# mLSTM and two-level expert layer on one core: first scores moved ahead of the end of the gate sums, gate tanh in 24 pieces, carried states in four tiles

## The chip, the cores and the metric

One NeuronCore of a Trainium2 chip runs the whole program. The metric is the device time of one execution in microseconds; a kernel's time is the median over several executions.

## What is computed

Two stages follow each other. An mLSTM (4 batches, 8 heads, 768 tokens, head size 40) makes one row of 320 numbers per token; 3072 such rows then go through a mixture of 16 experts, of which each token uses one.

```python
for t in range(S):                       # mLSTM, per batch and head
    m_new = max(f_gate[t] + m, i_gate[t])
    f_stab = exp(f_gate[t] + m - m_new); i_stab = exp(i_gate[t] - m_new)
    C = f_stab * C + i_stab * outer(v[t], k[t])
    n = f_stab * n + i_stab * k[t]
    y[t] = sigmoid(o_gate[t]) * (C @ q[t]) / max(abs(n @ q[t]), 1)
x = y as (3072, 320)
g = argmax(x @ w_group); e = argmax(x @ w_expert[g])
out = softmax_g * softmax_e * (relu(x @ w1[g, e]) @ w2[g, e])
```

## The kernel before

**Units.** The first stage does the recurrence in chunks of 128 tokens. One unit u is chunk c = u // 4 of batch b = u % 4, with all 8 heads, so there are 24 units, done in order. Inside a chunk the recurrence is a masked product, as in attention; across chunks each batch and head carries a state of 40 by 41 numbers (the extra column is n).

**What a unit does**, with the names that the profile shows:

- `scores(u)` (L218): TensorE makes keys times queries into the two PSUM tiles `sp`. Needs the transfer of `qk`.
- `decay(u, r)` for r = 0 and 1: `aprod` (L188, L191) makes four 128x128 decay exponents with TensorE into a PSUM bank `aw`, and `exps` (L201) turns them on ScalarE into half r of `ab` with four exponentials. In chunk 0 a matmul of `neg_b` (L188) comes first and masks. The pool `ps_a` has one buffer: a second `aw` can only be written when the four exponentials of the one before have read it. Three calls early in the program take the bank tagged `lg` instead.
- `masked(u, r)` (L223): VectorE multiplies `sp` by `ab` into `pt`.
- `carried(u)` (L243), from chunk 1 on: TensorE multiplies the queries by the carried state, read from `Cflat`, into the tile `it`. `carried2` (L250, VectorE) scales it by `eacol`. `it` also has one buffer; `state(u)` (L262) writes the chunk's contribution into its second half, and `state2(u)` (L277, L279; VectorE, one unit later) adds that to the state. `decayed(u)` (L269, GpSimd) scales the state.
- `values(u)` (L290): TensorE makes `av` from `pt` and the values `nt`.
- `norm1`, `rows`, `rows2` (L296 to L319), for unit u - 1: VectorE and GpSimd normalise and multiply by the output gate `sig`, giving `x`. `store` (L333, L334) copies a strip on ScalarE and writes the rows to DRAM. `turn` (L327, L350) transposes `x` on TensorE into the bank `tp` and copies it to `xT` on ScalarE. The bank `tp` too is single, and the gate sums use it as well.
- `gate_o(c)` (L169): tanh of the output gates of a chunk's four units in one ScalarE instruction of 128x1280, in place.

**Order.** Units 0 to 21 stand in an order written out by hand (`unit`), and each engine runs its own instructions in that order; a scheduler places only what comes after. In unit u stand, in this order: loads for u + 3, scores(u), the last part of unit u - 1, masked(u), carried(u), keyw(u + 1) (L230, GpSimd), decay(u + 2, 0), turn(u - 1), values(u), state(u), decay(u + 2, 1). After decay(u + 2, 1) of units 2, 6, 10, 14 and 18 comes `gate_o` of the next chunk.

**The start.** `gate_sums(0)` (L964 on) makes the cumulative gates of chunk 0 in five steps on VectorE and GpSimd, and last a transpose on TensorE into `tp` (L988) that gives `bcol`, the exponentials' bias. Before it TensorE runs 11 matmuls on ones (`busy`, L133). After it come decay(0, 0), decay(0, 1), scores(0), the rest of unit 0, then `unit(1, first=True)`, which also does both halves of decay(2). `gate_sums(1)` and `later_sums` do the later chunks' gates in between; after unit 2, and again after unit 6, `ends` (L1005) makes a matmul into `tp`, from which ScalarE makes `decs` with two copies (L1008).

After unit 23 the experts run, from L764 to L871 mostly; weights arrive in halves, are split into a rounded part and a rest, and three products are summed.

Of the kernel before, what the change touches and what calls it, by code (L numbers as in the profile page):

```python
# [7 lines left out]
F32 = mybir.dt.float32  # L8
# [3 lines left out]
AF = mybir.ActivationFunctionType  # L12
# [6 lines left out]
P = 128  # L19
B, H, S, D = 4, 8, 768, 40  # L20
NCH = S // P
NU = NCH * B
# [12 lines left out]
D1 = D + 1  # L35
Z = 64 - D
KS = 64 + D
HC = 4 * D1
# [26 lines left out]
def lstm_moe(ctx: ExitStack, tc: tile.TileContext, gates, qkT, nat, og, wcat, w1, w2, cst, out):  # L65
    nc = tc.nc
    enter = ctx.enter_context
    mm = nc.tensor.matmul
# [39 lines left out]
    ap_ = att_pool("att", 1)  # L108
# [2 lines left out]
    Apc = ap_.tile([P, S], BF16, name="Apc")  # L111
    sel_b = ap_.tile([P, B * H], BF16, name="sel_b")
    decs = ap_.tile([P, NCH, B * 4], F32, name="decs")
    Cflat = ap_.tile([P, B * HC + P - D1], F32, name="Cflat")
    Cst = Cflat[:, 0:B * HC].rearrange("p (a e) -> p a e", e=D1)
    kws = [ap_.tile([P, 4 * KS + Z], F32, name=f"kw{i}") for i in range(2)]
    rows_of = slice(0, 64), slice(64, 64 + D)
    bcol = ap_.tile([P, NCH, B * H], F32, name="bcol")
# [1 line left out]
    wk = att_pool("wk", 2)  # L120
# [40 lines left out]
    sigs = {}  # L161
# [3 lines left out]
        nc.sync.dma_start(t, og[:, c * B:(c + 1) * B, :])  # L165
        sigs[c] = t

    def gate_o(c):
        nc.scalar.activation(sigs[c], sigs[c], AF.Tanh, scale=0.5)  # L169

    def upper(a, fill):
        rt["mask"] = nc.gpsimd.affine_select(out=a, in_=a, pattern=[[0, a.shape[1]], [1, P]], compare_op=ALU.is_ge, fill=fill,
# [30 lines left out]
    def decay(u, r, **kw):  # L203
        aprod(u, r, **kw)
        exps(u, r)
# [5 lines left out]
    def scores(u):  # L211
        t = st_[u]
        qk = t["qk"]
        t["pm"] = [ps_s.tile([P, 4, P], F32, name="sp") for _ in range(2)]
        for pr in range(4):
            for r in range(2):
                rs = rows_of[r]
                mm(t["pm"][r][:, pr, :], qk[rs, 0, pr, :], qk[rs, 1, pr, :], start=True, stop=True)  # L218
# [15 lines left out]
    def carried(u):  # L234
        c, b = divmod(u, B)
        t = st_[u]
        it = t["it"] = ps_a.tile([P, 2, 512], F32, name="it")
        if c > 0:
            for pr in range(4):
                for r in range(2):  # L240
                    rs = rows_of[r]
                    o = (b * 4 + pr) * D1
                    mm(it[:, r, pr * D1:pr * D1 + P], t["qk"][rs, 1, pr, :], Cflat[rs, o:o + P], start=True, stop=True)  # L243

    def carried2(u):
        c, b = divmod(u, B)
# [18 lines left out]
    def decayed(u):  # L265
        c, b = divmod(u, B)
        if 0 < c < NCH - 1:
            cb = Cst[:, b * 4:b * 4 + 4, :]
            nc.gpsimd.tensor_tensor(cb, cb, bc(decs[:, c, b * 4:b * 4 + 4].unsqueeze(2), (P, 4, D1)), op=ALU.mult)  # L269

    def state2(u):
        c, b = divmod(u, B)
        if c < NCH - 1:
            st = st_[u]["it"][:, 1, HC:2 * HC].rearrange("p (a e) -> p a e", e=D1)
            cb = Cst[:, b * 4:b * 4 + 4, :]
            if c > 0:
                nc.vector.tensor_tensor(cb, cb, st, op=ALU.add)  # L277
            else:
                nc.vector.tensor_copy(cb, st)  # L279
# [58 lines left out]
    def turn(u):  # L338
        x = st_[u]["x"]
        tp = ps_1.tile([P, 3, P], F32, name="tp", tag="tp")  # L340
        ins = turned(tp, x, (0, P, DM - P))
        rt["tp", u] = ins
        if NU - 4 < u < NU - 1:
            with tc.issue_after(ins.ins):
                busy(2 if u == NU - 3 else 1)
        if u == NU - 1:
            xT = lasting().rearrange("p (k c) -> p k c", k=3)
        else:
            xT = wk.tile([P, 3, P], F32, name="xT", bufs=5)
        nc.scalar.copy(xT, tp)  # L350
        st_[u]["xT"] = xT
        if NU - 4 < u < NU - 1:
            with tc.issue_after(ins.ins):
                do(early_turns, 1)
# [526 lines left out]
    def run(stage, u):  # L881
        if 0 <= u < NU:
            stage(u)
# [12 lines left out]
    def unit(u, more=0, first=False):  # L896
        run(loads, u + 3)
        if u == 6:
            first_tokens()
        if u == 9:  # L900
            last_rows()
        if u % B == 1 and u // B + 1 < NCH:
            load_o(u // B + 1)
        with ExitStack() as st:
            if u == MANUAL:
                st.enter_context(tc.issue_after(rt["av", u - 1].ins))
            run(scores, u)
        if first:
            decay(2, 0)
            decay(2, 1, pool=ps_1, tag="lg")  # L910
        with ExitStack() as st:
            if u == NU:
                st.enter_context(tc.high_priority())
            run(norm1, u - 1)
            run(rows, u - 1)
            run(state2, u - 1)
            run(rows2, u - 1)
        if u in (17, 19, 20, 21):
            put_id()
        run(store, u - 1)  # L920
        run(mask, u + 1)
        run(lambda v: masked(v, 0), u)
        run(lambda v: masked(v, 1), u)
        run(carried, u)
        run(decayed, u)
        run(carried2, u)
        if u == MANUAL:
            with tc.issue_after(rt["num"].ins):
                go_on(9, "B")
        run(keyw, u + 1)  # L930
        run(lambda v: decay(v, 0), u + 2)
        if u < NU:
            run(turn, u - 1)
        if u < NU - 1:
            go_on(9 if u < MANUAL else 0, "A")
        elif u == NU - 1:
            with tc.issue_after(rt["tp", u - 1].ins):
                go_on(1, "A")
            with tc.issue_after(rt["num"].ins):
                go_on(3, "B")  # L940
            with tc.issue_after(rt["mask"].ins):
                while ids:
                    put_id()
            logits(u - 2)
            logits(u - 1)
            go_on(4, "B")
        if u == 5:
            first_rows()
        run(values, u)
        run(state, u)  # L950
        if u in ROUTE:
            logits_of(ROUTE[u], 0, B)
        run(lambda v: decay(v, 1), u + 2)
        if u < MANUAL:
            go_on(4 + more, "B")
        if u in ROUTE:
            logits_back(ROUTE[u], 0, B)
        if u % B == 2 and u // B + 1 < NCH:
            gate_o(u // B + 1)
        if u < MANUAL:  # L960
            put_id()

# [80 lines left out]
    def sum_on(n=1):  # L1043
        for _ in range(n):
            if sums and next(sums[0], StopIteration) is StopIteration:
                sums.pop(0)

    with tc.manual_schedule():
        nc.sync.dma_start(G[:, 0], gates[0:BH])
        nc.scalar.dma_start(cs, cst)  # L1050
        nc.scalar.dma_start(G[:, 1], gates[BH:2 * BH])
        nc.scalar.dma_start(G4, gates[2 * BH:])
        nc.vector.memset(ones_b, 1.0)
        nc.vector.memset(sep, 0.0)
        nc.scalar.activation(sep, sep, AF.Exp)
        busy(11)
        nc.vector.memset(ones4, 1.0)
        nc.vector.memset(Dl[:, 0, 0:1], 0.0)
        nc.vector.memset(Apc[96:P], 0.0)
        for t in qkp[0:2]:  # L1060
            nc.gpsimd.memset(t[0:Z], 0.0)
        load_qk(0)
        loads(0)
        load_o(0)
        load_qk(1)
        loads(1)
        loads(2)
        nc.scalar.copy(sel_b, cs[:, C_SEL:C_SEL + B * H])
        nc.scalar.copy(lt_b, cs[:, C_LT:C_LT + P])
        nc.scalar.activation(neg_b, ident, AF.Copy, scale=NEG)  # L1070
        sums.append(gate_sums(0))
        sum_on(9)
        for t in kws:
            nc.gpsimd.memset(t, 0.0)
        nc.gpsimd.memset(zero_b, 0.0)
        for t in qkp[2:]:
            nc.gpsimd.memset(t[0:Z], 0.0)
        nc.gpsimd.memset(Cflat, 0.0)
        nc.gpsimd.tensor_copy(id_b, ident)
        decay(0, 0)  # L1080
        decay(0, 1, pool=ps_1, tag="lg")
        scores(0)
        keyw(0)
        masked(0, 0)
        masked(0, 1)
        carried(0)
        carried2(0)
        sums.append(gate_sums(1))
        decay(1, 0)
        values(0)  # L1090
        gate_o(0)
        decay(1, 1, pool=ps_1, tag="lg")
        state(0)
        sum_on(3)
        keyw(1)
        nc.gpsimd.iota(tokid, pattern=[[P, NBLK], [0, IW]], base=0, channel_multiplier=1)
        nc.gpsimd.tensor_copy(keyb, cs[:, C_15E:C_15E + NE])
        nc.gpsimd.tensor_copy(base_b, cs[:, C_BASE:C_BASE + NE])
        nc.gpsimd.memset(ohsum[0], 0.0)
        loads(3)  # L1100
        nc.sync.dma_start(wc, wcat)
        unit(1, first=True)
        sum_on(9)
        sums.append(later_sums())
        sum_on(1)
        for u in range(2, 10):
            unit(u)
            do(due if u in (2, 6) else [])
            sum_on({2: 2, 3: 3, 4: 2, 5: 9}.get(u, 0))
# [113 lines left out]
    with tc.For_i(0, nv, 1):  # L1223
# [6 lines left out]
        v = wk2.tile([P, 3], F32, name="v")  # L1230
# [30 lines left out]
        for f in range(NF):  # L1261
            ps = pools["ps_h"].tile([P, 512], F32, name="psh")
            for k in range(3):
                kk = min(P, DM - k * P)
                mm(ps[:, 0:P], w1s[0:kk, k * F + f * P:k * F + (f + 1) * P], xT[0:kk, k, :], start=(k == 0),
                   stop=(k == 2))
# [74 lines left out]
```

## Time and profile before

| what | value |
|---|---|
| median of 3 executions | 391.44 us (389.32 to 392.74) |
| the profiled execution's own time | 389.26 us |
| its span in the profile | 387.7 us |
| TensorE busy | 368.8 us (95%) |
| VectorE busy | 274.1 us (71%) |
| ScalarE busy | 212.1 us (55%) |
| GpSimd busy | 171.1 us (44%) |
| granted TensorE clock, mean | 0.994 |

The profile is of one execution, 1.56 us longer by its own time than its span. PE is TensorE's matmuls, PEld its weight loads, DVE VectorE, ACT ScalarE, POOL GpSimd, SPq the queue that issues most transfers. In a timeline row stand start, length, engine, line, output and inputs; "[idle before <-releaser]" is how long that engine had nothing to run and what ended last before it. An fp32 matmul shows as two records, so 8 of them read x16. The first stage ends around 150 us.

### The profile page before, as it was taken

How to read it: one execution, taken by the hardware profiler on the slowest of the kernel's cores; microseconds unless marked ns; L12 is line 12 of the kernel's file. 1: busy time of each engine (PE TensorE's matmuls, PEld its weight loads, DVE VectorE, ACT ScalarE, POOL GpSimd, SP SyncE). 2: the span in 40 equal slices, each digit the busy share in tenths (PEclk: the TensorE clock that was granted, in tenths of full speed). 3: DMA queues.
4: the chain of work that ended last, by engine and by line, in shares of the span. 5: the costliest groups of instructions: out<-in, count | busy, mean ns of one | idle time of the engine just before them, and what ended most of it. 6: DMA issues, size and time to landing. Idle time of an engine off the chain costs nothing.

```text
span 387.7 us, 9816 instructions
## 1 busy us (share of the span) xinstructions
PE 368.8 (95%) x3688; PEld 339.9 (88%) x3688; DVE 274.1 (71%) x702; ACT 212.1 (55%) x533; POOL 171.1 (44%) x222
## 2 busy tenths in 40 slices
PE   7989999999999999877999999999999999999994
PEld 4778988979978888877999898999999998888993
DVE  5867876898898976786697767865755666656620
ACT  5664574565746532435675556755746745455520
POOL 7545486566767434374433216352141243141310
PEclk9999999999999999998999999999999999999999
DMA  7976856899795731149952369995862718988700
GB/s 230 264 244 171 206 164 193 301 325 280 208 332 133 221 85 44 15 121 356 374 181 65 103 249 385 407 319 199 315 229 80 265 43 318 332 342 294 251 18 10
DMA packets 29553, 84.05 MB, mean 217 GB/s; under 512 B 12168, under 2 KB 16754, under 8 KB 25922
## 3 DMA queue, kind: packets, MB, share of 16 engines
q1 hardware_dynamic: 24258, 66.41, 52.1%
q0 software_dynamic: 4912, 16.66, 12.7%
q8 instruction: 29, 0.48, 0.5%
q10 hardware_dynamic: 336, 0.36, 0.3%
q14 instruction: 18, 0.15, 0.1%
HBM read 73.11 MB, written 10.54 MB: 216 GB/s over the span
## 4 chain that ended last, share of the span: by engine, by line
PE 63%; issue 13%; DVE 11%; DMA 7%; POOL 2%; ACT 2%; POOLq 1%; SPq 0%; DVEq 0%; ACTq 0%
PE psh L816 13%; PE av L290 8%; PE po L857 5%; PE po L855 5%; PE po L856 5%; PE sp L218 4%; PE it L243 4%; PE tpm L327 2%; PE aw L191 2%; PE it L262 2%; DVE w2l L682 2%; PE tp L327 2%; DMA w2s<-in_w_dram 2%; PE psh L764 1%; DMA ix<-itab 1%
## 5 line engine op out<-in xcount | busy, mean ns | idle before, releaser
L201 ACT ACTIVATE ab<-aw,bcol 128x128 f32<-128x128 f32 x192 | 54.5, 371 | 41.9 <-PE aw L191 38.9
L622 POOL DMA_INDIRECT out_dram<-y,ix x32 | 38.1, 1190 | 88.9 <-ACT y L867 72.7
L855 PE MATMUL po<-w2h,hh 128*128 128x320 f32 (+3 forms) x200 | 63.4, 317 | 0.0
L857 PE MATMUL po<-w2h,hh 128*128 128x320 f32 (+3 forms) x200 | 62.2, 311 | 1.1 <-DVE hh L753 1.1
L856 PE MATMUL po<-w2l,hh 128*128 128x320 f32 (+3 forms) x200 | 61.9, 309 | 0.0
L618 POOL DMA_INDIRECT xg<-x_d,ix x32 | 34.3, 1073 | 49.2 <-DMA ix<-itab 27.2
L816 PE MATMUL psh<-xhl,w1hl 128*128 128x240 f32 (+5 forms) x336 | 54.0, 287 | 0.4 <-DVE hf L748 0.4
L682 DVE TENSOR_TENSOR w2l<-w2s,w2h 128x640 fp32r<-128x640 f32 x52 | 41.3, 833 | 15.4 <-ACT w2h L680 13.3
L750 ACT ACTIVATE hh<-psh 128x256 fp32r<-128x256 f32 (+5 forms) x68 | 28.8, 429 | 40.5 <-DVE hf L748 20.0
L753 DVE SCALAR_TENSOR_TENSOR hh<-psh,hh 128x256 fp32r<-128x256 f32 (+4 forms) x76 | 31.9, 442 | 24.0 <-ACT hh L750 22.8
L290 PE MATMUL av<-nt,pt 128*128 128x128 f32 x384 | 47.7, 276 | 0.5 <-DVE pt L223 0.5
L816 PEld LDWEIGHTS psh<-xhl,w1hl 128*128 128x128 f32 x336 | 46.3, 189 | 1.5 <-PE psh L816 0.9
L290 PEld LDWEIGHTS av<-nt,pt 128*128 128x128 f32 x384 | 45.1, 192 | 1.1 <-DVE pt L223 0.9
L223 DVE TENSOR_TENSOR pt<-sp,ab 128x512 f32<-128x512 f32 x48 | 30.9, 684 | 11.7 <-PE sp L218 11.1
L857 PEld LDWEIGHTS po<-w2h,hh 128*128 128x128 f32 (+3 forms) x200 | 36.6, 183 | 1.4 <-DVE hh L753 1.4
L855 PEld LDWEIGHTS po<-w2h,hh 128*128 128x128 f32 (+3 forms) x200 | 36.8, 184 | 0.5 <-ACT y L867 0.5
L867 ACT ACTIVATE y<-po,xg 128x320 f32<-128x320 f32 (+3 forms) x25 | 13.2, 529 | 43.9 <-PE po L857 43.7
L856 PEld LDWEIGHTS po<-w2l,hh 128*128 128x128 f32 (+3 forms) x200 | 36.8, 184 | 0.0
L764 PE MATMUL psh<-xhl,w1s 128*128 128x144 f32 (+7 forms) x336 | 36.0, 284 | 0.0
L680 ACT CAST w2h<-w2s 128x640 fp32r<-128x640 f32 x52 | 35.0, 724 | 0.9 <-DMA w2s<-in_w_dram 0.9
L764 PEld LDWEIGHTS psh<-xhl,w1s 128*128 128x128 f32 (+1 forms) x336 | 34.4, 190 | 1.1 <-issue 0.2
L526 POOL DMA_INDIRECT itab<-tokid,slot x24 | 25.7, 1070 | 17.5 <-DVE slot L449 7.5
(229 smaller groups left out, 728.6 us busy)
## 6 DMA issues: line engine op xcount, KB each, us to landing
w1s<-in_w_dram SPq DMA_DIRECT2D x12, 1536.0 KB
w2s<-in_w_dram SPq DMA_DIRECT2D x9, 1280.0 KB
nt<-in_nat_dram SPq DMA_DIRECT2D x24, 324.0 KB
qk<-in_qkT_dram SPq DMA_DIRECT2D x24, 320.0 KB
x_d<-x SPq DMA_DIRECT2D x23, 192.0 KB
sig<-in_og_dram SPq DMA_DIRECT2D x6, 640.0 KB
w1hl<-in_w_dram SPq DMA_DIRECT2D x3, 1280.0 KB
w1s<-in_w_dram SPq DMA_DIRECT2D x4, 768.0 KB
```

The lines of the kernel that those rows point to most:

```text
L201: rt["exp"] = nc.scalar.activation(st_[u]["ab"][:, r, j, :], aw[:, j, :], AF.Exp, bias=bcol[:, c, i:i + 1])
L290: ins = mm(av[:, i:i + P], t["pm"][r][:, pr, :], nt[:, o:o + P], start=True, stop=True)
L618: return nc.gpsimd.indirect_dma_start(out=o, out_offset=None, in_=src, in_offset=bass.IndirectOffsetOnAxis(ap=idx, axis=0))
L622: return nc.gpsimd.indirect_dma_start(out=out, out_offset=bass.IndirectOffsetOnAxis(ap=idx, axis=0), in_=y, in_offset=None, bounds_check=N ...
L680: nc.scalar.copy(a, src[:, s])
L682: lows.append(lambda: nc.vector.tensor_tensor(o[rows], src[rows, s], a[rows].bitcast(F32), op=ALU.subtract))
L753: rt['low'] = nc.vector.scalar_tensor_tensor(hh[:, f:f + per, dst], src[:, :, t], 0.0, hr.bitcast(F32)[:, :, t], op0=ALU.max, op1=ALU.subt ...
L764: return mm(banks[i][:, g * W1:(g + 1) * W1], w1s[rs, s:s + P], xhl[rs, k, :], **kw)
L816: ins = mm(ps[:, g * W1:(g + 1) * W1], w[:, s], x, start=(n == 0), stop=(n == len(todo) - 1))
L855: mm(po[0:m], hh[:, f, t], w2h[:, s], start=st0, stop=False)
L856: mm(po[0:m], hh[:, f, t], w2l[:, s], start=False, stop=False)
L857: ins = mm(po[0:m], hh[:, f, tl], w2h[:, s], start=False, stop=sp0)
```

## The change

1. The gate sums of chunk 0 run their five steps, then `scores(0)` is emitted, then the last step, the transpose and `bcol`. Before, scores(0) came after the transpose and after both halves of decay(0).
2. `gate_o` takes a unit instead of a chunk: one tanh of 128x320 per unit, 24 in all instead of 6. Unit 0's and unit 1's stand where their unit is written; from unit 1 on each unit u also does unit u + 1's, between its state matmuls and decay(u + 2, 1).
3. In unit 1 alone, values(1) and state(1) come ahead of turn(0) and decay(3, 0).
4. The carried states lie in four tiles, one for each batch, of 251 columns each, instead of one of 743. Each is cleared by its own memset.
5. `xT` has 4 buffers instead of 5.

```diff
-    Cflat = ap_.tile([P, B * HC + P - D1], F32, name="Cflat")
-    Cst = Cflat[:, 0:B * HC].rearrange("p (a e) -> p a e", e=D1)
+    Cst = [ap_.tile([P, HC + P - D1], F32, name=f"Cst{i}") for i in range(B)]
...
-    def gate_o(c):
-        nc.scalar.activation(sigs[c], sigs[c], AF.Tanh, scale=0.5)
+    def gate_o(u):
+        c, b = divmod(u, B)
+        nc.scalar.activation(sigs[c][:, b], sigs[c][:, b], AF.Tanh, scale=0.5)
...
-                    o = (b * 4 + pr) * D1
-                    mm(it[:, r, pr * D1:pr * D1 + P], t["qk"][rs, 1, pr, :], Cflat[rs, o:o + P], start=True, stop=True)
+                    o = pr * D1
+                    mm(it[:, r, o:o + P], t["qk"][rs, 1, pr, :], Cst[b][rs, o:o + P], start=True, stop=True)
...
-            xT = wk.tile([P, 3, P], F32, name="xT", bufs=5)
+            xT = wk.tile([P, 3, P], F32, name="xT", bufs=4)
...
         run(keyw, u + 1)
-        run(lambda v: decay(v, 0), u + 2)
-        if u < NU:
-            run(turn, u - 1)
+        if not first:
+            run(lambda v: decay(v, 0), u + 2)
+            if u < NU:
+                run(turn, u - 1)
...
         run(values, u)
         run(state, u)
+        if first:
+            turn(u - 1)
+            decay(u + 2, 0)
+            gate_o(u)
+        run(gate_o, u + 1)
...
-        if u % B == 2 and u // B + 1 < NCH:
-            gate_o(u // B + 1)
...
         sums.append(gate_sums(0))
+        sum_on(5)
+        scores(0)
         sum_on(9)
...
-        nc.gpsimd.memset(Cflat, 0.0)
+        for t in Cst:
+            nc.gpsimd.memset(t, 0.0)
         nc.gpsimd.tensor_copy(id_b, ident)
         decay(0, 0)
         decay(0, 1, pool=ps_1, tag="lg")
-        scores(0)
```

**TensorE at the start**, after the 11 matmuls on ones; `sp` is scores(0), `tp` the transpose for `bcol`, `aw` the decays of unit 0 and, at the end, of unit 1.

```order
-L988 MATMUL tp<-cs,G 128x32
...
+L218 MATMUL sp<-qk_93 128x128 x8
+L992 MATMUL tp<-cs,G 128x32
 L188 LDWEIGHTS lt_b
 L188 MATMUL aw<-neg_b,lt_b 128x512
...
 L191 LDWEIGHTS sel_b
 L191 MATMUL aw<-Apc,sel_b 128x128
-L218 MATMUL sp<-qk_93 128x128 x8
 L188 LDWEIGHTS lt_b
```

The eight score matmuls stood behind both decays and now stand ahead of the transpose.

**TensorE in unit 1**, behind the decays of unit 2; `av` is values(1), `it` state(1), `tp` turn(0), and the two `aw` groups are decay(3, 0) and decay(3, 1).

```order
 L191 LDWEIGHTS sel_b
 L191 MATMUL aw<-Apc,sel_b 128x128
+L290 MATMUL av<-nt,pt 128x128 x8
+L262 MATMUL it<-nt,kw_105 64x41 x8
+L327 MATMUL tp<-cs,x 128x128 x3
 L188 LDWEIGHTS lt_b
...
-L327 MATMUL tp<-cs,x 128x128 x3
-L290 MATMUL av<-nt,pt 128x128 x8
-L262 MATMUL it<-nt,kw_102 64x41 x8
 L188 LDWEIGHTS lt_b
 L188 MATMUL aw<-neg_b,lt_b 128x512
```

turn(0), values(1) and state(1) stood between the two halves of decay(3); now all three stand ahead of both, and the halves follow each other directly.

**ScalarE from unit 1's copy of `xT` to the copies of `decs` after unit 2.** `ab` are groups of four exponentials. First as it was:

```order
L350 COPY xT<-tp 128x384
L201 ACTIVATE ab<-aw,bcol 128x128 x4
L998 ACTIVATE eacol<-tp 128x32
L999 COPY bcol<-tp 128x32
L333 COPY x<-x 128x64
L201 ACTIVATE ab<-aw,bcol 128x128 x4
L350 COPY xT<-tp 128x384
L201 ACTIVATE ab<-aw,bcol 128x128 x4
L169 ACTIVATE sig<-sig 128x1280
L1008 COPY decs<-tp 64x16 x2
```

Now the exponentials of decay(3, 0) come behind `xT`:

```order
L350 COPY xT<-tp 128x384
L201 ACTIVATE ab<-aw,bcol 128x128 x4
L169 ACTIVATE sig<-sig 128x320 x2
L201 ACTIVATE ab<-aw,bcol 128x128 x4
L1002 ACTIVATE eacol<-tp 128x32
L1003 COPY bcol<-tp 128x32
L333 COPY x<-x 128x64
L201 ACTIVATE ab<-aw,bcol 128x128 x4
L350 COPY xT<-tp 128x384
L169 ACTIVATE sig<-sig 128x320
L201 ACTIVATE ab<-aw,bcol 128x128 x4
L1012 COPY decs<-tp 64x16 x2
```

The tanh of a whole chunk no longer stands between the exponentials and the copies of `decs`; two small ones stand between the exponentials of decay(3, 0) and of decay(3, 1), and one ahead of those of decay(4, 1). The tanh of the last unit, 23, lies outside the hand-written order; the scheduler puts it on ScalarE in unit 17, right behind that of unit 18. On TensorE, VectorE, GpSimd and SP nothing else changes its place.

## Prediction before the result

> **What bounds the kernel now.** The page first: the engines' busy time and the chain of work that ended last.
>
> ```profile
> PE 368.8 (95%) x3688; PEld 339.9 (88%) x3688; DVE 274.1 (71%) x702; ACT 212.1 (55%) x533; POOL 171.1 (44%) x222
> PE 63%; issue 13%; DVE 11%; DMA 7%; POOL 2%; ACT 2%; POOLq 1%; SPq 0%; DVEq 0%; ACTq 0%
> ```
>
> TensorE is busy nearly throughout, and ScalarE, which most of the change touches, holds 2% of the chain. A reordering can win only what TensorE stands idle in the first stage. The busy time by stages tells how much that is; the start's row:
>
> ```profile
> 5.20:27.00 21.80, 19.04 (x227) 15.97 (x227) 15.76 (x45) 15.08 (x52) 12.29 (x23) 1.00 0.96 273
> ```
>
> The second column is the length of the stretch, the third TensorE's busy time in it: 2.76 us idle between 5.2 and 27 us, at the full granted clock (1.00). The waits of TensorE name the holes, first those of 13 to 28 us, then those of 27 to 130 us: a wait, its sum, its count, the longest.
>
> ```profile
> PE tp L327 <- POOL ab L172: 1.0, 1, 1.0
> PE aw L188 <- ACT ab L201: 0.8, 1, 0.8
> ```
>
> ```profile
> PE it L243 <- DVE Cflat L277: 1.5, 4, 0.6
> PE tp L327 <- POOL x L319: 0.2, 1, 0.2
> ```
>
> So there are two holes near the moved instructions, 0.8 and 1.0 us, and later a third kind, 1.5 us in four pieces, before the matmuls on the carried state. The change touches the surroundings of all three.
>
> **Part A, scores(0) ahead.** The start, from the timelines of TensorE, SP, ScalarE and VectorE, and what SP's queue waited for:
>
> ```profile
> 1.26 3.98 PE L133 MATMUL busy<-ones_b 128*128 128x512 bf16 x11 [1.26 <-DVE sep L1054]
> 5.41 0.24 PE L988 MATMUL tp<-cs,G 32*128 32x32 f32 x1 [0.16 <-POOL G L977]
> 5.58 0.39 PE L188 MATMUL aw<-neg_b,lt_b 128*128 128x512 bf16 x1
> 6.26 0.38 PE L191 MATMUL aw<-Apc,sel_b 128*128 128x128 bf16 x4 [0.29 <-POOL Apc L985]
> 7.02 1.16 PE L218 MATMUL sp<-qk 64*128 64x128 f32 x16
> 8.11 0.39 PE L188 MATMUL aw<-neg_b,lt_b 128*128 128x512 bf16 x1
> 8.34 0.39 PE L191 MATMUL aw<-Apc,sel_b 128*128 128x128 bf16 x4
> 9.03 2.05 PE L290 MATMUL av<-nt,pt 128*128 128x128 f32 x16 [0.31 <-DVE pt L223]
> 10.92 0.38 PE L188 MATMUL aw<-neg_b,lt_b 128*128 128x512 bf16 x1
> 5.05 0.33 SPq L181 DMA_DIRECT2D nt<-in_nat_dram  x1
> SPq L181 <- DMA qk<-in_qkT_dram: 0.3, 1, 0.3
> 6.68 3.22 ACT L201 ACTIVATE ab<-aw,bcol 128x128 f32<-128x128 f32 x12 [2.20 <-PE aw L191]
> 8.29 1.30 DVE L223 TENSOR_TENSOR pt<-sp,ab 128x512 f32<-128x512 f32 x2 [2.00 <-PE sp L218]
> ```
>
> The matmuls on ones end at 1.26 + 3.98 = 5.24. SP's issue at 5.05 had waited for the transfer of the first keys, so these lie ready at about 5.0, just in time. scores(0) then runs from 5.24 for 1.09 (7.02 to 8.11), to 6.33. The transpose, until now at 5.41, goes to 6.33. The masking matmul follows it 0.17 later (5.41 to 5.58), the decay that 0.23 later (8.11 to 8.34) where it need not wait for the gates, as it did at 6.26; by 6.7 these are long ready. So the first decay runs from 6.73 to 7.11, where it was done at 6.64, and the exponentials begin at 7.15 instead of 6.68. Four of them take 1.14, so the first product `pt` can begin at 8.33, against 8.29 when it waited for the scores. The second needs all eight (2.17, from the row of eight below) and begins at 9.36, where it began 0.65 after the first, at 8.94. From a product's start to the matmuls that await it pass 0.74 (8.29 to 9.03). values(0) starts at 9.07, is half through after 0.95 (half of 9.03 to 10.92), at 10.02, then waits for the second `pt` until 10.10, and ends at 11.04 instead of 10.92. **Part A: 0.1 us lost**, and VectorE 0.45 us behind. Bounds: 0.2 won if the second product is not awaited; 1.8 lost (7.02 - 5.24) if the keys are not there before 7.02, which is all that the old place proves by itself. I take the 0.1, since SP's wait dates the keys.
>
> **Part B, unit 1.**
>
> ```profile
> 9.50 0.51 DVE L969 TENSOR_TENSOR_SCAN M__126<-G,M__126 32x128 f32<-32x128 f32 x1
> 13.24 1.29 DVE L223 TENSOR_TENSOR pt<-sp,ab 128x512 f32<-128x512 f32 x2
> 13.79 2.17 ACT L201 ACTIVATE ab<-aw,bcol 128x128 f32<-128x128 f32 x8 [1.09 <-PE aw L191]
> 14.99 0.38 PE L188 MATMUL aw<-neg_b,lt_b 128*128 128x512 bf16 x1 [0.79 <-ACT ab L201]
> 15.76 1.95 PE L290 MATMUL av<-nt,pt 128*128 128x128 f32 x16
> 17.64 0.67 PE L262 MATMUL it<-nt,kw 128*64 128x41 f32 x16
> 18.24 0.39 PE L188 MATMUL aw<-neg_b,lt_b 128*128 128x512 bf16 x1
> 19.02 1.16 PE L218 MATMUL sp<-qk 64*128 64x128 f32 x16
> 16.95 0.56 ACT L350 COPY xT<-tp 128x384 f32<-128x384 f32 x1
> ```
>
> Until now decay(3, 0) waited 0.79 for the single bank `aw`, held until the first four exponentials of unit 2 were through (13.79 + 1.14). values(1), state(1) and turn(0) now go into that gap. But VectorE bounds values(1): from L969 to the product `pt` it worked 3.74 us without a pause (9.50 to 13.24), and it now begins 0.45 late, so `pt` starts at 13.70 and, with the 0.74, values(1) at 14.44. It takes 1.88 and state(1) 0.60 (from start to start above), turn(0) 0.36 (26.65 to 27.01 in part C): 17.28. decay(3, 0) is done 0.23 + 0.39 later, at 17.90. And now the same bank bites harder: decay(3, 1) comes next, with nothing between, and must wait for four exponentials, from 17.95 (after the copy of `xT`) to 19.09. It starts at 19.15, 0.06 behind them as at 14.99, and scores(2) 0.78 later as before, at 19.93 instead of 19.02. **Part B: with A 0.91 lost, so 0.81 by itself.** The work that used to hide this wait (turn, values and state, 2.8 us) stands before it now. Bounds: the wait cannot shrink below the 1.14 of the exponentials, so without any slip on VectorE 0.6 is lost; with the 0.56 of `xT` wholly in front of them, 1.3.
>
> The tanh of units 1 and 2 stands between those exponentials and the next four. From the slope between the 1286 ns of 1280 columns and the 371 of 128 (rows in part D), 320 columns take 0.52 us, and 0.41 from start to start. Two put the exponentials of decay(3, 1) at 19.8 to 20.9; decay(4, 0) wants their bank at 21.0, behind scores(2). That hides them, barely.
>
> The Trainium skill (ScalarE: Activation LUTs, Rules for kernel authors) budgets about 0.3 us per ACTIVATE plus 0.83 ns an element, which speaks against cutting one into four; an estimate from it is 0.57 for a piece. By that budget the two pieces would end 0.3 later and the sum would come out 0.2 to 0.3 us slower than by the rows. The trace agrees on the long form (1.29 against 1.36), but starts short ones every 0.26 us (twelve in 3.22), so the row's figure is the one I use.
>
> **Part C, no long tanh after unit 2.**
>
> ```profile
> 24.04 1.14 ACT L201 ACTIVATE ab<-aw,bcol 128x128 f32<-128x128 f32 x4 [1.94 <-PE aw L191]
> 25.05 1.29 ACT L169 ACTIVATE sig<-sig 128x1280 f32<-128x1280 f32 x1
> 26.21 0.34 ACT L1008 COPY decs<-tp 64x16 f32<-64x16 f32 x2
> 24.22 0.72 POOL L319 TENSOR_TENSOR x<-xn,den 128x320 f32<-128x320 f32 x1 [3.38 <-DVE xn L310]
> 25.23 0.39 PE L191 MATMUL aw<-Apc,sel_b 128*128 128x128 bf16 x4
> 25.39 1.29 DVE L223 TENSOR_TENSOR pt<-sp,ab 128x512 f32<-128x512 f32 x2 [1.01 <-PE sp L218]
> 26.65 0.52 PE L327 MATMUL tp<-cs,x 128*128 128x128 f32 x3 [1.03 <-POOL ab L172]
> 27.01 1.95 PE L290 MATMUL av<-nt,pt 128*128 128x128 f32 x16
> ```
>
> The profile names GpSimd's mask for the 1.03 us. It is another: turn(2) needs `x`, done at 24.94, and the bank `tp`, which the `decs` copies held to 26.55; they stood behind the tanh. That tanh goes. All this is 0.91 late from part B: turn(2) could start at 25.62 + 0.91 = 26.53 (the end of decay(5, 0)), and the copies end at 24.95 + 1.01 + 0.34 = 26.30, so it does not wait. values(3) now waits for its `pt` instead: 25.39 + 0.91 + 0.74 = 27.04. It used to start at 27.01. **Part C gives back 0.88 of 1.03**; more than that only if `pt` were earlier, and nothing if something else held turn(2) to its old delay.
>
> **Part D, what costs nothing.**
>
> ```profile
> L169 ACT ACTIVATE sig<-sig 128x1280 f32<-128x1280 f32 x6 | 7.7, 1286 | 0.0
> L201 ACT ACTIVATE ab<-aw,bcol 128x128 f32<-128x128 f32 x184 | 52.2, 371 | 40.1 <-PE aw L191 37.1 <-PE tp L327 2.5 <-ACT x L333 0.3
> L1078 POOL MEMSET Cflat<- x1: 707/707/707, 9.0 to 9.0; 128x743 f32 x1
> ```
>
> 24 pieces at 0.41 are 9.8 us of ScalarE against 7.0 for six at 1.16: 2.8 us more. Each stands just ahead of exponentials before which ScalarE idled, 40.1 us in 46 groups, so they are hidden; without that cover the 18 after unit 4 would cost up to 7. The other long ones win nothing by going: after 27 us TensorE waits for no ScalarE row. Four memsets clear 1004 columns for 743, some 0.3 us at the 707 ns, ahead of the weighted keys that state(0) awaits; those have as much slack, and if not, state(0) moves by 0.1. The fifth `xT` buffer was never needed: the logits of a chunk read its four ahead of the next turn.
>
> The state tiles free nothing either. carried(u) waits for L277 of the unit before, of another batch. But `it`, which it writes, has one buffer, and the same L277 reads it: the wait stays. Bounds: 0, and 1.5 won.
>
> **Sum.** +0.10 + 0.81 - 0.88 = +0.03 us, that is none, on the profiled execution's 389.26. That one lay 2.2 below the median of the runs shown; the difference carried to the median gives **391.4**. The terms' bounds give -0.4 to +1.3.
>
> **Rivals.** (1) Both holes close: neither bank nor VectorE makes a new wait, -0.79 - 1.03 = -1.8, 389.6. For it: the rows show both holes and the order removes what filled them. Against: the single `aw`. (2) Slower, by the keys: scores(0) now heads TensorE's line and everything stands behind it, so each 0.1 us that they land after 5.24 costs 0.1. They have 0.2 of slack by the one row; a slip of 1.1 would give 0.9, 392.3. (3) The state tiles do free carried(u): -1.5, 389.9. For it: the row names the state; against: `it`. (4) The last unit's tanh, now in unit 17 (about 113 us), waits there for a transfer issued at unit 17's start and holds back exponentials: some 0.5 us, 391.9, if it comes more than 1 us later than ScalarE gets there.
>
> **How the numbers follow.** The forecast 0.55, rival 1 0.20, rival 2 0.15, rivals 3 and 4 0.05 each. The terms' bounds alone make 391.0 to 392.7. The executions shown reach 2.1 below their median and 1.3 above it; the range 389.0 to 393.2 takes in rival 1's 389.6 and the upper bound with half a microsecond of that scatter at each end. About 1% (3.9 us) can be told from no change; no case reaches it, and the holes are not that large. So 0.92 for within 1%, and 0.04 on each side for what a placement further on might do.
>
> **What would show it.** Right: scores(0) at 5.2 and the first exponentials near 7.15; a hole of over 1 us ahead of decay(3, 1) near 18; scores(2) near 19.9; none before turn(2); values(3) near 27.0; carried(u) waiting for VectorE as before. Wrong: scores(2) at or before 19.0 (rival 1), scores(0) after 5.5 (rival 2), no wait at carried(u) (rival 3), or values(3) off by over 0.5.

## The result and the profile after

| | changed | before, same chip | ratio, with its 95% interval |
|---|---|---|---|
| median | 393.56 us (391.17 to 395.35) | 390.95 us (389.32 to 393.46) | 1.0061 (1.0044 to 1.0077) |
| profiled execution, own time | 393.08 us | 389.26 us | |
| its span | 391.3 us | 387.7 us | |

The change makes the kernel 0.6% slower, some 2.4 us by the ratio (the two medians differ by 2.6; losses below go by the ratio), where 391.4 us and no change were forecast. TensorE at the start and in units 1 to 3 of the changed kernel, as a timeline (start, length, what, idle before it):

```profile
5.27 1.16 PE L218 MATMUL sp<-qk 64*128 64x128 f32 x16
14.40 2.05 PE L290 MATMUL av<-nt,pt 128*128 128x128 f32 x16
19.20 0.38 PE L188 MATMUL aw<-neg_b,lt_b 128*128 128x512 bf16 x1 [1.23 <-ACT ab L201]
19.97 1.16 PE L218 MATMUL sp<-qk 64*128 64x128 f32 x16
26.38 0.52 PE L327 MATMUL tp<-cs,x 128*128 128x128 f32 x3
26.95 2.05 PE L290 MATMUL av<-nt,pt 128*128 128x128 f32 x16
```

scores(0) runs at 5.27, values(1) at 14.40, the hole ahead of decay(3, 1) is 1.23 us, scores(2) comes at 19.97, turn(2) waits for nothing, and values(3) starts at 26.95. The prediction had 5.24, 14.44, over 1, 19.93, none, 27.04. The start and its three terms are as forecast, so the loss is elsewhere. The waits of TensorE from 105 to 130 us, in the changed kernel and then in the kernel before (a wait, its sum, count, longest), name the place:

```profile
PE it L243 <- DVE Cst L277: 1.4, 3, 0.8
PE aw L191 <- ACT ab L201: 1.4, 1, 1.4
```

```profile
PE it L243 <- DVE Cflat L277: 0.9, 3, 0.4
```

One wait is new: a decay that waits 1.4 us for exponentials. ScalarE there, in the changed kernel and then before:

```profile
113.49 0.51 ACT L169 ACTIVATE sig<-sig 128x320 f32<-128x320 f32 x1
117.00 0.47 ACT L169 ACTIVATE sig<-sig 128x320 f32<-128x320 f32 x1 [3.01 <-DMA sig<-in_og_dram]
117.38 1.13 ACT L201 ACTIVATE ab<-aw,bcol 128x128 f32<-128x128 f32 x4
```

```profile
114.65 1.14 ACT L201 ACTIVATE ab<-aw,bcol 128x128 f32<-128x128 f32 x4 [1.19 <-PE aw L191]
```

The first tanh is unit 18's; the second is unit 23's, which the scheduler had put into unit 17. ScalarE is done with the first at about 114.0 and then stands before it for 3.01 us, until the transfer of chunk 5's gates has landed. Behind it stand the exponentials of decay(19, 1): 117.38 instead of 114.65. The chain of waits of the changed kernel between 105 and 130 us, in order of time, runs through just these:

```profile
107.67 9.25 DMA sig<-in_og_dram
...
117.00 0.23 ACT sig L169
...
117.38 1.14 ACT ab L201 x4
...
118.55 0.38 PE aw L191 x4
```

The piece "DMA" is 9.25 us long: the transfer was issued at 107.67 and landed at 116.92. Before the change the same transfer is issued at the same place, and nobody waits for it, as the long tanh stands a unit later.

How the 3.01 us become a loss: decay(20, 0) needs the bank that these exponentials read. TensorE's rows of decay(20, 0) and carried(21), in the changed kernel and then before:

```profile
118.55 0.38 PE L191 MATMUL aw<-Apc,sel_b 128*128 128x128 bf16 x4 [1.35 <-ACT ab L201]
124.22 1.16 PE L243 MATMUL it<-Cst,qk 64*128 64x128 f32 x16 [0.78 <-DVE Cst L277]
```

```profile
117.02 0.40 PE L191 MATMUL aw<-Apc,sel_b 128*128 128x128 bf16 x4
122.22 1.16 PE L243 MATMUL it<-Cflat,qk 64*128 64x128 f32 x16 [0.30 <-DVE Cflat L277]
```

The decay is 1.53 late; the two programs are 0.11 apart in the rows ahead of it, so 1.42 are lost. VectorE's next piece adds to it, with GpSimd beside it (a row of each in the changed kernel, then the same two before):

```profile
120.17 0.64 DVE L449 CAST slot<-slf 128x4 int32<-128x4 f32 x1
```

```profile
120.05 0.74 POOL L230 TENSOR_TENSOR kw<-nt,ab 128x320 f32<-128x320 f32 x1
```

```profile
118.65 0.17 DVE L449 CAST slot<-slf 128x4 int32<-128x4 f32 x1
```

```profile
117.87 0.73 POOL L230 TENSOR_TENSOR kw<-nt,ab 128x320 f32<-128x320 f32 x1
```

A cast of four columns took 0.64 instead of 0.17 us: GpSimd's weighted keys, delayed by the same exponentials, now run beside it, and it ends when they end (120.81 and 120.79). The state's update L277 follows from that, and carried(21) is 2.00 late, 0.1 of it from before this place. Next, TensorE waits 0.66 us for the experts' first gather, where it waited 0.18 (changed, then before):

```profile
143.32 0.52 PE L327 MATMUL busy<-cs,xg 128*128 128x128 f32 x3 [0.66 <-DMA xg<-x_d,ix]
```

```profile
140.83 0.52 PE L327 MATMUL busy<-cs,xg 128*128 128x128 f32 x3 [0.18 <-DMA xg<-x_d,ix]
```

That gives 0.1 + 1.4 + 0.5 + 0.5 = 2.5, against the 2.4 of the ratio. Only the 1.4 and the first 0.5, together 1.9, follow from the stall by these rows. The gather's 0.5 is not shown to follow from it: below, dam has the stall and waits 0.29 us there, while pin and pin2 have none and wait 0.51 and 0.55. The two profiled spans differ by 3.6; the other 1.1 lie in the experts, where this execution had a granted clock of 0.94 from 145 to 200 us against 0.97. The stall does not decide that clock: pin and ahead below, without the loss, show 0.94 there, pin2, the same kernel as pin, 0.97, and deep, with the longest stall, 0.97.

### The profile page after: what moved, and what is told of

It reads as the page before. It is cut to its first block, busy times and chain, and to the rows that moved or that the text cites. A ratio compares the mean times of both kernels' runs of the same rounds, so it can differ in the third digit from the quotient of the medians.

```text
span 391.3 us, 9830 instructions
## 1 busy us (share of the span) xinstructions
PE 370.8 (95%) x3688; PEld 341.7 (87%) x3688; DVE 274.9 (70%) x702; ACT 214.8 (55%) x551; POOL 173.9 (44%) x225
## 4 chain that ended last, share of the span: by engine, by line
PE 71%; issue 9%; DMA 7%; DVE 6%; ACT 3%; POOL 2%; POOLq 1%; SPq 0%; DVEq 0%; ACTq 0%
PE psh L816 12%; PE av L290 10%; PE po L857 6%; PE po L855 6%; PE po L856 6%; PE psh L764 5%; PE sp L218 5%; PE it L243 3%; PE tpm L327 3%; PE it L262 3%; PE aw L191 2%; DMA sig<-in_og_dram 2%; PE tp L327 2%; DMA w2s<-in_w_dram 2%; PE po L847 2%
## 5 line engine op out<-in xcount | busy, mean ns | idle before, releaser
L618 POOL DMA_INDIRECT xg<-x_d,ix x32 | 36.5, 1141 | 51.9 <-DMA ix<-itab 26.6
L857 PEld LDWEIGHTS po<-w2h,hh 128*128 128x128 f32 (+3 forms) x200 | 37.0, 185 | 1.6 <-DVE hh L753 1.6
L855 PEld LDWEIGHTS po<-w2h,hh 128*128 128x128 f32 (+3 forms) x200 | 37.3, 186 | 0.5 <-ACT y L867 0.5
```

Of the source, the lines that this page charges most:

```text
L618: return nc.gpsimd.indirect_dma_start(out=o, out_offset=None, in_=src, in_offset=bass.IndirectOffsetOnAxis(ap=idx, axis=0))
L855: mm(po[0:m], hh[:, f, t], w2h[:, s], start=st0, stop=False)
L857: ins = mm(po[0:m], hh[:, f, tl], w2h[:, s], start=False, stop=sp0)
```

## The experiments

Two theories. **Q**: all of the loss is ScalarE's queue standing behind the transfer in unit 17; the rest of the change nets nothing. **P**: the 24 pieces, the state tiles and the new start cost it, spread over the program.

**pin: the late tanh kept in its place.**

```diff
-        run(gate_o, u + 1)
+        if u < MANUAL:
+            gate_o(u + 1)
+        if u == MANUAL - 1:
+            gate_o(NU - 1)
```

> The changed kernel with unit 23's tanh kept in unit 21 of the hand-written order, behind that of unit 22; nothing else moves. Theory Q (the whole loss is ScalarE's queue standing behind the transfer of chunk 5's gates in unit 17): ScalarE no longer idles 3.0 us at 113.9, decay(20, 0) starts near 117.1 where it started at 118.55, the score matmuls' later rows come 2.0 us earlier, and the time is that of the kernel before within 0.2%, 390.4 to 391.7 us (ratio 0.9985 to 1.002). Rival P (the 24 pieces, four state tiles or the new start cost it spread over the program): still slower by 0.4 to 0.8%, some 393 us.

391.45 us against 390.39, ratio 1.0011 (0.9982 to 1.0040). ScalarE in unit 17:

```profile
113.96 0.51 ACT L169 ACTIVATE sig<-sig 128x320 f32<-128x320 f32 x1
115.25 1.14 ACT L201 ACTIVATE ab<-aw,bcol 128x128 f32<-128x128 f32 x4 [0.78 <-PE aw L191]
```

The stall is gone; the exponentials wait for TensorE again. decay(20, 0) starts at 117.61 in a program that began 0.6 us later (scores(0) at 5.89), so at 117.0. P falls as an account of the loss. The same kernel on another chip:

> The kernel of pin once more (the change with unit 23's tanh kept in unit 21), to narrow its interval: Theory Q says that the rest of the change nets nothing, a ratio of 0.998 to 1.002 with an interval that holds 1; if early scores(0) or the hole ahead of decay(3, 1) cost more than the sum had, 1.002 to 1.004.

388.47 against 388.36, ratio 1.0009 (0.9990 to 1.0028). Both intervals hold 1, and the ratios stand for 0.3 to 0.4 us above it: the rest of the change nets nothing that these runs can tell.

**dam: the stall alone, put into the kernel before.**

```diff
+        if u == 17:
+            gate_o(5, 3, 4)
...
-            gate_o(u // B + 1)
+            gate_o(u // B + 1, 0, 3 if u == 18 else B)
```

(gate_o here takes a chunk, the first of its units to do and the one to stop ahead of.)

> The kernel before with one thing of the change: unit 23's quarter of chunk 5's tanh (128x320) stands in unit 17 behind the copy of xT, the other three quarters stay where the long one was. Theory Q: the same idle ScalarE of about 3 us until the gates' transfer lands near 117, carried(21) late by 2.0, and 0.4 to 0.8% slower, 392.7 to 394.0 us. Rival P: a fifth tanh instruction costs 0.4 us at most, so at most 391.4 us and a ratio under 1.0015.

391.94 against 390.39, ratio 1.0048 (1.0020 to 1.0076). ScalarE, then TensorE's rows for decay(20, 0) and carried(21):

```profile
116.98 0.47 ACT L169 ACTIVATE sig<-sig 128x320 f32<-128x320 f32 x1 [3.09 <-DVE pt L223]
```

```profile
118.53 0.38 PE L191 MATMUL aw<-Apc,sel_b 128*128 128x128 bf16 x4 [1.01 <-ACT ab L201]
124.19 1.16 PE L243 MATMUL it<-Cflat,qk 64*128 64x128 f32 x16 [0.77 <-DVE Cflat L277]
```

The profile names VectorE's `pt` as the releaser; VectorE had long been done, and the end, 116.98, is that of the transfer in the changed kernel. This program began 0.4 us late and still goes on at the same 118.53 and 124.19: the landing, not the program, sets the time. The move of one instruction of 0.47 us, without anything else of the change, gives 1.9 us by the ratio: the 1.4 and the 0.5 above, and, within the noise, the size of the change's whole loss.

**ahead: the transfer earlier, the tanh still early.**

```diff
-        if u % B == 1 and u // B + 1 < NCH:
+        if u % B == 1 and u < 17:
...
+            if u == 16:
+                load_o(5)
             do(early_loads, {10: 2, 11: 1, 12: 1, 15: 1, 16: 1, 19: 1, 20: 1}.get(u, 0))
```

> The changed kernel with the transfer of chunk 5's gates issued at the end of unit 16, ahead of a weight transfer (w1s) that stood in front of it, so some 3 us earlier; unit 23's tanh stays early on ScalarE, and now falls one place further forward, behind the exponentials at 108.4. Theory Q with the queue as the cause: the transfer lands before 110.5, where ScalarE has nothing to do until 112.1, so no exponential is late: 390.4 to 391.7 us, ratio 0.9985 to 1.002. If instead the early place of the tanh itself costs (its own 0.4 us or the buffer's release), the loss stays at 0.4% or more.

391.59 against 390.39, ratio 1.0034 (1.0006 to 1.0062). ScalarE:

```profile
111.69 0.47 ACT L169 ACTIVATE sig<-sig 128x320 f32<-128x320 f32 x1 [2.32 <-DVE pt L223]
112.07 0.23 ACT L333 COPY x<-x 128x64 f32<-128x64 f32 x1
112.20 1.13 ACT L201 ACTIVATE ab<-aw,bcol 128x128 f32<-128x128 f32 x4
```

The expected landing was missed: not before 110.5, but at about 111.6, 7.3 us after its issue at 104.35. Here too ScalarE stood 2.32 us before the tanh, yet it had nothing to do but until 112.1, so the exponentials start 0.1 later than in the changed kernel, and every later row of TensorE down to unit 22's scores (137.38 against 137.39) is within 0.02 us of where it was before the change. The rows are as Q has them: a stall that holds back nothing costs nothing up to there. The timing does not decide. The ratio lies between Q's 1.002 and the 1.004 of the rival, and its interval overlaps both pin's and the change's. What the 0.3% are, if anything, stays open.

**deep: the same wait made longer.**

```diff
         run(keyw, u + 1)
+        if u == 17:
+            gate_o(NU - 1)
         if not first:
...
-        run(gate_o, u + 1)
+        if u < MANUAL:
+            gate_o(u + 1)
```

> The changed kernel with unit 23's tanh one place further forward in unit 17, ahead of the exponentials of decay(19, 0), so ScalarE reaches it near 110.8 and waits for the same transfer (landing near 116.9) some 6 us instead of 3. Theory Q: decay(19, 0)'s exponentials end near 118.3 instead of 113.2, decay(20, 0) starts near 120.4 instead of 118.55, and the time is 1.5 to 2.5 us above the changed kernel's, 394.8 to 396.5 us, ratio 1.010 to 1.014. Rival P: the place is of no account, ratio 1.004 to 1.008 as for the change.

395.75 against 390.39, ratio 1.0147 (1.0109 to 1.0185): 5.7 us lost, so 3.3 more than by the change, where 1.5 to 2.5 were expected (the time itself lies inside its range, the ratio just above). ScalarE stood 5.78 us, and TensorE shows why the price was too low:

```profile
118.56 0.58 PE L191 MATMUL aw<-Apc,sel_b 128*128 128x128 bf16 x4 [3.92 <-ACT ab L201]
119.08 2.08 PE L218 MATMUL sp<-qk 64*128 64x128 f32 x16
```

Here follows the stretch with the hole in it: length, TensorE's busy time and, third from the end, the granted clock.

```profile
113.00:125.00 12.00, 8.08 (x84) 7.45 (x83) 5.47 (x16) 5.78 (x20) 5.44 (x10) 0.72 0.36 127
```

After an idle 3.92 us the scores took 2.08 instead of 1.16. The clock granted from 113 to 125 was 0.72 on the mean, and 0.50 from 118.5 to 124, where it had been 1.00 up to 113. After the change's 1.35 us it stayed at 1.00 (119 to 125 in the changed kernel). The Trainium skill (TensorE: Matmul & The Clock Gate, The HAM clock gate) gives half the clock after an idle window of about 3.4 us; these two holes lie on either side of it and agree. The loss grows with the wait, which P did not have, but not in proportion.

**moves, pieces: the prediction's terms one at a time.** moves is the kernel before with the moves of scores(0), values(1), state(1) and turn(0) only. pieces, further down, is the kernel before with the 24 tanh only, the last kept in unit 21.

```diff
-        run(lambda v: decay(v, 0), u + 2)
-        if u < NU:
-            run(turn, u - 1)
+        if not first:
+            run(lambda v: decay(v, 0), u + 2)
+            if u < NU:
+                run(turn, u - 1)
...
         run(state, u)
+        if first:
+            turn(u - 1)
+            decay(u + 2, 0)
...
+        sum_on(5)
+        scores(0)
         sum_on(9)
...
         decay(0, 1, pool=ps_1, tag="lg")
-        scores(0)
```

> The kernel before with the moves on TensorE alone: scores(0) ahead of the transpose, values(1), state(1) and turn(0) ahead of decay(3, 0); the long tanh and the one state tile stay. By the terms of the prediction: the wait for the bank aw ahead of decay(3, 1) is 1.2 us, scores(2) starts 0.9 later than before, the hole of about 1.0 ahead of turn(2) stays, since the long tanh and everything around it move along, and values(3) is 0.8 to 0.95 later than before from the same start. If the moves alone cost nothing, values(3) stays at 27.0.

```profile
6.04 1.16 PE L218 MATMUL sp<-qk 64*128 64x128 f32 x16 [0.84 <-DMA qk<-in_qkT_dram]
19.78 0.38 PE L188 MATMUL aw<-neg_b,lt_b 128*128 128x512 bf16 x1 [1.23 <-ACT ab L201]
20.54 1.16 PE L218 MATMUL sp<-qk 64*128 64x128 f32 x16
28.19 0.52 PE L327 MATMUL tp<-cs,x 128*128 128x128 f32 x3 [1.04 <-POOL ab L172]
28.54 1.73 PE L290 MATMUL av<-nt,pt 128*128 128x128 f32 x14
```

In this execution the keys landed late, so everything began 0.77 after the 5.27 of the changed kernel. Taken off, scores(2) is at 19.77 and values(3) at 27.77: 0.75 and 0.76 later than before, a little less than expected. Both holes stand, 1.23 and 1.04. One execution took 389.22 us.

```diff
-    def gate_o(c):
-        nc.scalar.activation(sigs[c], sigs[c], AF.Tanh, scale=0.5)
+    def gate_o(u):
+        c, b = divmod(u, B)
+        nc.scalar.activation(sigs[c][:, b], sigs[c][:, b], AF.Tanh, scale=0.5)
...
         run(state, u)
+        if first:
+            gate_o(u)
+        if u < MANUAL:
+            gate_o(u + 1)
+        if u == MANUAL - 1:
+            gate_o(NU - 1)
...
-        if u % B == 2 and u // B + 1 < NCH:
-            gate_o(u // B + 1)
```

> The kernel before with the tanh of each unit in a piece of its own, the last one kept in unit 21 of the written order; the start, unit 1 and the state tiles stay as before. By the terms of the prediction: the long tanh no longer stands ahead of the copies of decs, so the 1.03 us before turn(2) goes and values(3) starts near 26.1 instead of 27.0 (counted from the same start), and nothing else changes: 0.9 us faster, ratio 0.9977 (0.996 to 0.9995). If 18 more instructions on ScalarE cost by themselves, unit 10's scores are not 0.9 earlier than before but level or later.

387.23 against 388.75, ratio 0.9963 (0.9943 to 0.9984). values(0) and turn(2), values(3):

```profile
9.75 2.05 PE L291 MATMUL av<-nt,pt 128*128 128x128 f32 x16 [0.31 <-DVE pt L224]
26.14 0.52 PE L328 MATMUL tp<-cs,x 128*128 128x128 f32 x3
26.71 2.05 PE L291 MATMUL av<-nt,pt 128*128 128x128 f32 x16
```

It began 0.72 late (9.75 against 9.03). Taken off, values(3) is at 25.99, 1.02 earlier than before. The long tanh cost about what the prediction said. Of the lead 0.91 is left at scores(4) (29.62 against 29.81) and 0.84 at scores(10) (66.09 against 66.21), so 18 more instructions on ScalarE cost less than 0.1 there.

**lead, lead2, lead3: closing the hole that the moves opened.** lead is the changed kernel with the late tanh kept in unit 21, decay(3, 1) in the bank tagged `lg`, unit 1's tanh behind unit 0's and unit 2's behind the exponentials of decay(3, 1).

```diff
-            gate_o(u)
-        run(gate_o, u + 1)
+        elif u < MANUAL:
+            gate_o(u + 1)
+        if u == MANUAL - 1:
+            gate_o(NU - 1)
...
-        run(lambda v: decay(v, 1), u + 2)
+        if first:
+            decay(u + 2, 1, pool=ps_1, tag="lg")
+            gate_o(u + 1)
+        else:
+            run(lambda v: decay(v, 1), u + 2)
...
         gate_o(0)
+        gate_o(1)
```

> The changed kernel with unit 23's tanh kept in unit 21, and the hole that the prediction's part B made closed: decay(3, 1) takes the bank tagged lg, unit 1's tanh stands behind unit 0's, and unit 2's behind the exponentials of decay(3, 1). By the terms: scores(2) 1.2 us earlier than in the changed kernel (18.75 instead of 19.97, from the same start), values(2) 0.8 to 1.2 earlier, no idle ScalarE in unit 17, so 0.8 to 1.2 us below the kernel before: ratio 0.997 to 0.998. If something else then waits in unit 2 (the bank tp, VectorE), values(3) is at most 0.4 earlier and the ratio 0.999 to 1.001.

387.45 against 388.75, ratio 0.9979 (0.9956 to 1.0002): where it was expected, with an interval that still holds 1.

```profile
18.49 1.16 PE L218 MATMUL sp<-qk 64*128 64x128 f32 x16
20.76 0.52 PE L327 MATMUL tp<-cs,x 128*128 128x128 f32 x3 [0.77 <-ACT x L333]
21.11 1.95 PE L290 MATMUL av<-nt,pt 128*128 128x128 f32 x16
```

scores(2) is 1.5 us earlier than in the changed kernel and values(2) 0.8 (21.11 against 21.91): the rest is given back ahead of turn(1), as the bank `tp` is held by the gate sums' copies, which stand behind the exponentials of decay(3, 1). lead2 moves that step forward:

```diff
             turn(u - 1)
             decay(u + 2, 0)
+            sum_on(9)
...
         unit(1, first=True)
-        sum_on(9)
```

> The version lead with one more move: the last step of gate_sums(1), its two transposes into tp and the two ScalarE copies from it, stands ahead of decay(3, 1) instead of behind it, so tp is free again before turn(1). In lead turn(1) stood 0.77 us idle for it. From the same start: scores(2) 0.2 to 0.3 later than in lead (the transposes wait for the copy of xT), turn(1) without a wait, values(2) 0.4 to 0.6 earlier than in lead, values(3) as much: 1.2 to 1.5 us below the kernel before, ratio 0.996 to 0.997. If something else waits in its place, values(3) is within 0.2 of lead's and the ratio stays at 0.998.

386.79 against 388.36, ratio 0.9947 (0.9927 to 0.9968): faster than the kernel before and than the changed one.

```profile
5.84 1.16 PE L218 MATMUL sp<-qk 64*128 64x128 f32 x16
20.58 0.50 PE L327 MATMUL tp<-cs,x 128*128 128x128 f32 x3
21.26 2.05 PE L290 MATMUL av<-nt,pt 128*128 128x128 f32 x16 [0.18 <-DVE pt L223]
26.30 2.05 PE L290 MATMUL av<-nt,pt 128*128 128x128 f32 x16
```

From the same start as lead (0.49 off) values(2) is at 20.77, 0.34 earlier and a little less than the 0.4 expected; values(3) is at 25.81, against 26.05 in lead. lead3 is lead2 with scores(0) back behind the decays of unit 0:

```diff
-        sum_on(5)
-        scores(0)
         sum_on(9)
...
         decay(0, 1, pool=ps_1, tag="lg")
+        scores(0)
```

> The version lead2 with part A undone: scores(0) goes back behind the decays of unit 0. By the terms of the prediction part A put VectorE 0.45 us behind and bought nothing, and it exposes the program to a late landing of the first keys (0.84 us idle in the look at the moves alone). So: the products of unit 1 0.3 to 0.45 earlier than in lead2 from the same start, values(3) 0.2 to 0.45 earlier, and the time 0.2 to 0.8 us below lead2's. If the early scores do help, it is slower than lead2.

387.05 against 388.36, ratio 0.9961 (0.9936 to 0.9986), where 0.2 to 0.8 us less than lead2 was expected; the two are not distinguishable. values(3):

```profile
25.69 2.05 PE L290 MATMUL av<-nt,pt 128*128 128x128 f32 x16
```

With the transpose at 5.37, it began as the kernel before; lead2, counted from scores(0) at 5.27, has 25.73. The 0.2 to 0.45 expected is 0.04: the early scores neither help nor hurt that these runs can tell.

## Why the prediction was wrong

**What was right.** What bounds the kernel; part A (first exponentials at 7.19 for 7.15); part B, 0.81 by itself and 0.91 with A (moves: 0.75 with A); part C, 0.88 given back (pieces: 1.02 when nothing else is late); the pieces of the tanh in the written order (0.51 us where 0.52 was forecast, two in 0.84) free of charge; the state tiles without effect on carried(u), which still waits 0.59, 0.25 and 0.37 us at 79.5, 110.0 and 116.0. pin is the sum of these, and it nets nothing that can be told, as the +0.03 said. Rival 2, keys that land late, did happen, but to one execution: of eight profiled ones with early scores, only the one of moves waited long for them (0.84 us). That the keys were there in time in the changed kernel's trace is no proof that they always are.

**The step that failed is part D, which put all the pieces at nothing, and with it the price of the fourth rival.** Part D let each piece be hidden by the idle time ahead of the exponentials that follow it. That holds for a tanh whose gates are there; unit 23's were not, so the tanh waited and the exponentials with it. The mechanism was written down as rival 4: the last unit's tanh waits in unit 17 for a transfer and holds back exponentials, "some 0.5 us, 391.9, if it comes more than 1 us later than ScalarE gets there", with a chance of 0.05. ScalarE got there at 114.0, where the text had "about 113 us", and the transfer landed 2.9 us later. The loss was not 0.5 but 1.9 us (1.4 ahead of decay(20, 0), 0.5 on VectorE; dam, the stall alone, 1.9). The price was never worked out from rows; it was the one term of the text without any. The rows were there. In the kernel before SP issued, from 100.79 to 107.55, two halves of weights, two units' keys and values, one store and then the gates, in KB 2 x 768, 2 x 320, 2 x 324, 192 and 640, or 3.7 MB. The stretches of that trace give what the DMA engines moved (last column, GB/s; before it their busy share):

```profile
100.80:107.50 6.70, 6.70 (x114) 6.13 (x116) 5.90 (x12) 3.62 (x12) 5.17 (x7) 1.00 0.93 269
107.50:116.90 9.40, 8.73 (x128) 7.45 (x116) 8.89 (x24) 5.22 (x18) 6.24 (x11) 1.00 0.91 312
```

1.8 MB of it were through by 107.5; the other 1.9 at 312 GB/s take 6.2 us, so by this estimate the gates cannot be there before 113.7, and if the 0.5 MB issued at 110.75 and 111.19 share the engines, not before 115.4. It was 116.9. The other half of the price is slack. decay(20, 0) stood at 117.02; less 1.14 for the four exponentials and the prediction's own 0.41 for the tanh, a landing up to 115.5 costs nothing, and each 0.1 us after that costs 0.1. The changed kernel gives the same: from the landing to decay(20, 0) pass 1.63 us (116.92 to 118.55), and 1.42 were lost. By the rows of before alone the landing thus lay at the edge of that slack with nothing that bounded it from above. That is a term with a lower end of 0 and an open upper one, and no rival at 0.05.

The range failed for the same reason: its -0.4 to +1.3 come from parts B and C (0.6 - 1.03 and 1.3 - 0, with part A's 1.8 left to rival 2), and no term stood in it for a ScalarE instruction that waits for a transfer.

**Open.** Whether the 0.3% of ahead is more than scatter; and what makes the gather's longer wait (0.66): without the stall pin, pin2 and pieces show 0.51, 0.55 and 0.52 there and ahead 0.24, with it dam shows 0.29. So up to 0.5 of the change's 2.4 us has no shown cause; by its interval, 1.7 to 3.0 us, the loss could also be no more than the stall's 1.9.

## What to carry to other kernels

When a change splits an instruction into pieces, look where every piece ends up, the last one above all if it lies outside a written order: here the scheduler put it into the unit in which its data are issued, ahead of work that was ready, on an engine that let nothing past it. Price such a wait by the landing of its transfer, summed from all bytes issued ahead of it and the rate that the trace shows, less the slack of what stands behind it. Moving the piece back is what is shown to help (pin, pin2); moving the transfer ahead was left undecided by its times. The version that keeps the piece late and frees the two single banks of units 1 and 2 (lead2) is 0.5% faster than the kernel before, where the change was 0.6% slower. How much of that the banks give is not settled: the small pieces alone give 0.4% (pieces), and the two intervals overlap.

## What the runs showed of the hardware

- A 640 KB transfer landed 9.25 us after its issue while the DMA engines were busy throughout (share 1.01, 327 GB/s), and 7.3 us after it when issued 3.3 us earlier, ahead of 768 KB of weights.
- ScalarE does not pass a waiting instruction: with ready exponentials behind it, it stood 3.01 us (5.78 in deep). The Trainium skill (TensorE: Matmul & The Clock Gate, the table at its head) says that ScalarE's queue is a strict FIFO; the traces agree.
- An idle 3.92 us of TensorE cost the clock (0.50 granted over the 5.5 us after it, in deep), an idle 1.35 us did not (1.00).
- The eleven matmuls on ones at the start took 3.86 us (ahead) to 4.88 us (dam), and the first keys landed up to 0.8 us later (moves) than in the changed kernel's profile, so whole programs are shifted by up to 0.8 us from one execution to the next. Rows of different executions are to be compared from the same start.
- A VectorE cast of 128x4 beside GpSimd's product of 128x320 took 0.64 instead of 0.17 us, and ended with it.
